# Attention and feed-forward in one kernel: copies of the weights issued earlier, sums of weights stored in fewer transfers, and a planned order made anew

## The chip, the core and the metric

The kernel runs on one core of a Trainium2 chip. The metric is device time in microseconds (us). The kernel before takes 865.53 us, the median of three runs (864.79 to 868.05).

## What is computed

Eight batches of attention with linear cost (softmax of q over its features, softmax of k over the sequence), eight heads of 64 features, 576 tokens. Its result is the input x (4608 x 512) of a feed-forward part with squared relu.

```python
q_s = exp(q - max(q, axis=-1));  q_s = q_s / sum(q_s, axis=-1)
k_s = exp(k - max(k, axis=2));   k_s = k_s / sum(k_s, axis=2)
kv = einsum('bhsd,bhse->bhde', k_s, v)
x = einsum('bhsd,bhde->bhse', q_s, kv)      # heads side by side: 4608 x 512
g = maximum(x @ w_in, 0) ** 2               # w_in 512 x 2048
out = g @ w_out                             # w_out 2048 x 512
```

## The kernel before, in words

**Exactness.** Each fp32 factor is split into a high and a low part (fp32r), and a product is three matmuls: high by high, low by high, high by low.

**Tiles and blocks.** The tokens make nine blocks of 512: 512 of the 576 of each batch, and a ninth of the 64 left over from each. Attention goes by pairs of heads, four to a block: `2.3` is pair 3 of block 2. Blocks 0 to 2 are multiplied plainly: step n (16 to a block, one for each chunk of 128 columns of w_in) has four pieces `h` of three matmuls each, then relu, square and split of the result (`relu`, `rm`, `ghi`, `glo`), and four pieces `o` that add to the output. Blocks 3 to 8 are taken two at a time in three wide passes `s0`, `s1`, `s2`, with seven products for each pair of chunks in place of eight (`A11`, `S4`, `S2`, `A12`, `S3`, `S1`, `A22`); the products need sums and differences of the weights and of the inputs. For a wide pass the weights don't fit beside the rest: each tile of 512 KB is read again from DRAM (`s0.R.5`, function `refill`, line 981).

**Where those copies come from.** The weights are first read in ORDER's steps. Later `own` (the unit `WA` of a pair of chunks, line 1028) stores three quarters of two w_in tiles, three transfers of 256 KB; `save` (units `W12`, `W34`, line 1020) stores the high and low parts of the sums, which DVE, POOL and ACT make before (units `a1` to `l34` of `w0` to `w7`); `keep_out` (`keep.n`, line 969) stores a w_out tile, 512 KB, 13 of them; `bring_back` (line 972) fetches four of them ahead of the first wide pass.

**One pair of heads**, units in turn: `Lk`, `Lq`, `Lv` load k, q and v; `km`, `k1`, `k2`, `ke`, `kx` and `qm`, `qd`, `qx`, `qs`, `qy` are the two softmaxes on DVE, POOL and ACT; `tb` turns q's tile on DVE, `Bw` writes it to DRAM (bounce) and `B` reads it back as qT, four DMAs into one tile; `kv` is the product of k and v; `kr` (with rs and kf), `kh` and `kl` scale and split it (kvs, ACT high, DVE low); `qh` and `ql` split qT (qs, ACT and POOL); `P0` to `P3` multiply the two, and `c`, `d`, `xh`, `xl`, `XL`, `XR` take the result as x.

**Inputs of a wide pass.** `x0.LB22` and its kin (line 1056) load half a block of x from DRAM; `x0.T10` to `x0.T41` are differences on DVE, `x0.hT2..` casts on ACT, `x0.lT2..` low parts on DVE. T1, T2, T3 use B22 or what was made of it; the product S2 uses T2.

**What sets the order.** Every engine works strictly in the order in which its instructions are written (class `InOrder`, line 284). That order is two tables of names: ORDER (from line 51) for blocks 0 and 1 and the start of 2, written by hand, and LIST (from line 91) for the rest, a planner's. All DMAs but a few are issued by SP, and an issue can't go before the ones ahead of it. `relu` and `square` (lines 876, 883) test BEGIN (line 43): from that step on the result stays in the bank and ACT squares it; before, it goes to SBUF and DVE squares it. All engine instructions have one line, that of the helper (294 before, 295 after), so the profile is read by tiles.

Of the kernel before, what the change touches and what calls it, by code (L numbers as in the profile page):

```python
# [1301 lines left out]
```

## Time and profile before

| | |
|---|---|
| median of three runs | 865.53 us (864.79 to 868.05) |
| the profiled execution | 863.45 us |
| its span on the core | 861.7 us |
| TensorE (PE) busy | 97% of the span |
| VectorE (DVE), ScalarE (ACT), GpSimd (POOL) busy | 64%, 57%, 33% |
| DMA, mean | 209 GB/s |
| TensorE's granted clock | 0.999 of full speed |

1.75 us of the profiled execution lie outside the span, and it is 2.08 us shorter than the median of the runs. In the profile's rows PE is TensorE's matmul, PEld its weight load, SPq the issue of DMAs by SP. An arrow points from input to output: `kvs<-kf` writes kvs from kf. A time in brackets is idle time before an instruction, with what ended it.

### The profile page before, as it was taken

What the parts mean: (1) busy time and instruction counts of PE and PEld (TensorE: products, weight loads), DVE (VectorE), ACT (ScalarE), POOL (GpSimd) and SP (SyncE); (2) the same over time, 40 slices, a digit from 0 to 9 for tenths busy, and PEclk for the clock granted to TensorE, in tenths of its full rate; (3) what the DMA queues carried; (4) which work ended last, traced back from release to release, by engine and by line L of the source; (5) the groups of instructions that cost most, each with busy time, mean ns of one, the idle gap of its engine ahead of it and who ended that gap; (6) DMA issues with size and microseconds to landing.
All of it is one profiled execution on the core that took longest, in us unless ns stands there. A gap on an engine that the chain in (4) does not pass through costs nothing.

```text
span 861.7 us, 13013 instructions
## 1 busy us (share of the span) xinstructions
PE 838.3 (97%) x4286; PEld 677.9 (79%) x4286; DVE 552.3 (64%) x1155; ACT 491.9 (57%) x932; POOL 288.0 (33%) x275
## 2 busy tenths in 40 slices
...
GB/s 232 294 167 310 202 75 151 273 231 277 225 231 245 271 267 289 233 301 253 252 265 263 278 173 170 236 175 168 147 242 198 102 215 147 166 162 161 175 70 49
DMA packets 136819, 179.66 MB, mean 209 GB/s; under 512 B 50864, under 2 KB 103088, under 8 KB 136752
## 3 DMA queue, kind: packets, MB, share of 16 engines
...
## 4 chain that ended last, share of the span: by engine, by line
PE 73%; DVE 10%; DMA 6%; SPq 4%; issue 3%; ACT 2%; POOL 1%; DVEq 0%; POOLq 0%; ACTq 0%
PE bank L294 73%; SPq L294 4%; DVE m L294 2%; DMA qt<-in_q_dram 1%; DMA raw_o<-in_moe_w_out_dram 1%; DMA kt<-in_k_dram 1%; DVE g_lo L294 1%; DMA xl_B<-x_raw 1%; DVE qm L294 1%; POOL qn L294 1%; DMA vt<-in_v_dram 1%; ACT bank L294 1%; DMA raw_i<-in_moe_w_in_dram 1%; DVE w L294 1%; DVE qs L294 1%
## 5 line engine op out<-in xcount | busy, mean ns | idle before, releaser
L294 PE MATMUL bank<-wp,g 128*128 128x512 f32 x648 | 160.8, 390 | 0.0
L294 PEld LDWEIGHTS bank<-wp,g 128*128 128x128 f32 x648 | 120.8, 188 | 25.3
L294 PE MATMUL bank<-x_hi,wi 128*128 128x512 f32 x384 | 131.8, 398 | 0.2 <-DVE g_lo L294 0.2
L294 PE MATMUL bank<-xh_T,wp 128*128 128x512 f32 x384 | 131.5, 392 | 0.0
L294 PE MATMUL bank<-wo,g_hi 128*128 128x512 f32 x384 | 121.0, 396 | 0.0
L294 POOL TENSOR_TENSOR qs<-qT,qs 64x640 fp32r<-64x640 f32 (+1 forms) x40 | 64.2, 1604 | 107.8 <-ACT qs L294 88.3
L294 PE MATMUL bank<-xh_B,wp 128*128 128x512 f32 x288 | 97.9, 390 | 0.0
L294 DVE TENSOR_TENSOR c<-c,bank 128x512 f32<-128x512 f32 x48 | 33.0, 687 | 95.8 <-ACT c L294 95.7
L294 PEld LDWEIGHTS bank<-x_hi,wi 128*128 128x128 f32 x384 | 72.2, 188 | 16.9 <-DVE g_lo L294 0.6
L294 ACT ACTIVATE far<-far 128x512 f32<-128x512 f32 x96 | 60.5, 631 | 42.7 <-DVE far L294 41.4
L294 PEld LDWEIGHTS bank<-xh_T,wp 128*128 128x128 f32 x384 | 72.1, 188 | 16.2 <-ACT bank L294 1.0
L294 PEld LDWEIGHTS bank<-wo,g_hi 128*128 128x128 f32 x384 | 69.8, 188 | 14.5 <-ACT g_hi L294 0.4
L294 PE MATMUL bank<-wo,g_lo 128*128 128x512 f32 x192 | 75.3, 392 | 0.0
L294 PE MATMUL bank<-x_lo,wi 128*128 128x512 f32 x192 | 75.0, 391 | 0.0
L294 PE MATMUL bank<-xl_T,wp 128*128 128x512 f32 x192 | 74.8, 390 | 0.0
L294 PE MATMUL bank<-wo_back,g 128*128 128x512 f32 x288 | 72.0, 391 | 0.0
L294 DVE TENSOR_TENSOR far<-far,bank 128x512 f32<-128x512 f32 x48 | 32.8, 684 | 50.5 <-PE bank L294 50.2
L294 DVE TENSOR_TENSOR g<-far,g 128x512 fp32r<-128x512 f32 x48 | 36.8, 806 | 43.9 <-ACT g L294 43.8
L294 PEld LDWEIGHTS bank<-xh_B,wp 128*128 128x128 f32 x288 | 54.1, 188 | 11.6
L294 PEld LDWEIGHTS bank<-wo_back,g 128*128 128x128 f32 x288 | 53.5, 188 | 11.3
L294 PE MATMUL bank<-xl_B,wp 128*128 128x512 f32 x144 | 56.2, 390 | 0.0
L294 POOL TENSOR_TENSOR qn<-qn,qs 128x640 f32<-128x640 f32 x30 | 38.2, 1274 | 52.1 <-DVE qs L294 28.9
(136 smaller groups left out, 1521.3 us busy)
## 6 DMA issues: line engine op xcount, KB each, us to landing
wp<-w_prod SPq DMA_DIRECT2D x84, 512.0 KB, 4.2
wp<-w_outs SPq DMA_DIRECT2D x54, 512.0 KB, 4.3
...
raw_i<-in_moe_w_in_dram SPq DMA_DIRECT2D x16, 512.0 KB, 6.1
raw_o<-in_moe_w_out_dram SPq DMA_DIRECT2D x16, 512.0 KB, 7.3
...
qT<-bounce SPq DMA_DIRECT2D x96, 80.0 KB, 2.9
w_outs<-wo SPq DMA_DIRECT2D x13, 512.0 KB, 3.6
```

Of the source, the lines that this page charges most:

```text
L294: ins = f(*args, **kwargs)
```

## The change

It has four parts. (1) BEGIN goes from 18 to 16, so the results of steps 16 and 17 are squared by ACT in the bank instead of by DVE in SBUF. (2) The copy of w_in gets another layout: own chunks in `w_own`, sums in `w_sums`, where high and low parts of two sums lie so that one DMA stores the high and one the low parts; a refill of a w tile then is two DMAs of 256 KB instead of one of 512 KB. (3) ORDER gets the units WA0 to WA5 and eight `ko` (keep_out) among the steps of block 1 and 2's start, and some output copies and stores (`ev`, `S`) stand earlier. (4) LIST is made anew. The units WA0 to WA7 and all 13 `keep` remain in LIST.

```diff
-BEGIN = 18
+BEGIN = 16
...
-rr13 kvn13 s2i13 rm11 lowo14 Lv21 to11 o8_2 o9_2 ghi10 ghi11 h12_0:0 h12_1 h12_2 h12_3 rc13 qmul13 s1o11 s2o11 ti14
+rr13 kvn13 s2i13 rm11 lowo14 Lv21 WA0 WA1 to11 o8_2 o9_2 ghi10 ghi11 h12_0:0 h12_1 h12_2 h12_3 rc13 qmul13 s1o11
...
-h15_2 h15_3 Lv22 ghi13 relu14 to14 s1o14 s2o14 to15 glo13 o13_3 o13_1 o13_2 hio14 loo14 o13_0 s1o15 s2o15 hio15 rm14
-ghi14 glo14 h16_0:1 relu15 rm15 ghi15 glo15 Bw20 Lk23 o14_3 qsub21 at13:3 loo15 o15_3 xhi13 xlo13 o14_0 o15_0 B20
-rs20 h16_1 rr20 qexp21 qn21 ev0 Bw21 h16_2 o14_1 o15_1 ev1 qh20 ql20 kf20 h16_3 relu16 rm16 B21 ev3 o14_2 o15_2 ev2
-ghi16 S2 glo16 Lq23 kh20 kl20 S0 S3 h17_0:3 h17_1 h17_2 h17_3 S1 relu17 rm17 ghi17 glo17
+h15_0:3 h15_1 h15_2 h15_3 Lv22 WA2 WA3 ko0 ko1 ko2 ghi13 relu14 to14 s1o14 s2o14 to15 glo13 o13_3 o13_1 o13_2 hio14
+loo14 o13_0 s1o15 s2o15 hio15 rm14 ghi14 glo14 h16_0:1 relu15 rm15 ghi15 glo15 Bw20 Lk23 WA4 ko3 ko4 ko6 ko7 o14_3
+qsub21 at13:3 loo15 o15_3 xhi13 xlo13 o14_0 o15_0 B20 rs20 h16_1 rr20 qexp21 ev3 S3 qn21 ev0 S0 WA5 ko8 Bw21 h16_2
+o14_1 o15_1 ev1 qh20 ql20 kf20 h16_3 relu16 rm16 ghi16 S1 B21 glo16 o14_2 o15_2 ev2 S2 kh20 kl20 Lq23 h17_0:3 h17_1
+h17_2 h17_3
...
 LIST = """
-P0/2.0 qm/2.2 w0.a2 w0.WA h18_0 c0/2.0 h18_1 d0/2.0 qd/2.2 km/2.2 P1/2.0 h18_2 c1/2.0 h18_3 d1/2.0 w0.s1 Lq/3.0
+w0.a2 w0.s1 qm/2.2 P0/2.0 h18_0 relu17 km/2.2 qd/2.2 h18_1 rm17 h18_2 ghi17 c0/2.0 h18_3 glo17 qx/2.2 o.16.0 d0/2.0
...
-    w_prod = dram.tile([len(used) // 2, P, 2, 2, 2 * P], F32, name="w_prod")
+    w_own = dram.tile([NPR, P, 3, 2, 2 * P], F32, name="w_own")
+    w_sums = dram.tile([NPR, 2, P, 2, 2, 2 * P], F32, name="w_sums")
...
         if kind == "w":
-            e.sp.dma_start(t.bitcast(F32), w_prod[i])
-            for k in range(2):
-                held[s, used[2 * i + k]] = t[:, k]
+            for k, (j, name) in enumerate(used[2 * i : 2 * i + 2]):
+                held[s, (j, name)] = t[:, k]
+                if name[0] == "A":
+                    src = w_own[j, :, ("A11", "A12", "A22").index(name)]
+                else:
+                    n, m = divmod(int(name[1]) - 1, 2)
+                    src = w_sums[j, n, :, :, m]
+                e.sp.dma_start(t[:, k].bitcast(F32), src)
...
         def save(n, src):
-            for i in range(2):
-                pair, place = divmod(w_at[j, f"S{2 * n + i + 1}"], 2)
-                e.sp.dma_start(w_prod[pair, :, place, 0], m[n][:, i].bitcast(F32))
-                e.sp.dma_start(w_prod[pair, :, place, 1], m[src][:, i])
+            e.sp.dma_start(w_sums[j, n, :, 0], m[n].bitcast(F32))
+            e.sp.dma_start(w_sums[j, n, :, 1], m[src])
...
+    parts = {f"w{j}": sum_units(j) for j in range(NPR)}
+    for j in range(NPR):
+        units[f"WA{j}"] = parts[f"w{j}"]["WA"]
+    for fc in range(NFC):
+        units[f"ko{fc}"] = lambda fc=fc: keep_out(fc)
     for token in ORDER:
```

How the change moves instructions, at three places. The rows are an engine's instructions in their order, each with its line, output, inputs and shape; "x4" is four alike in a row.

*SP at the end of ORDER*, from the v loads of block 2's third pair to the second fetch of qT. Before:

```order
L294 DMA vt_80<-in_v_dram 64x4x64
L294 DMA bounce<-tb 128x640
L294 DMA kt_79<-in_k_dram 64x2x320
L294 DMA kt_79<-in_k_dram 64x2x256
L294 DMA qT<-bounce 32x4x160 x4
L294 DMA bounce<-tb 128x640
L294 DMA qT<-bounce 32x4x160 x4
L294 DMA out_dram<-o 64x512 x2
```

In the changed kernel (the rows up to the stores after the first fetch):

```order
L295 DMA w_outs<-wo_713 128x1024
L295 DMA bounce<-tb 128x640
L295 DMA kt_79<-in_k_dram 64x2x320
L295 DMA kt_79<-in_k_dram 64x2x256
L295 DMA w_own<-wi_994 128x2x256 x2
L295 DMA w_own<-wi_1063 128x2x256
L295 DMA w_outs<-wo_798 128x1024
L295 DMA w_outs<-wo_878 128x1024
L295 DMA w_outs<-wo_1023 128x1024
L295 DMA w_outs<-wo_1094 128x1024
L295 DMA qT<-bounce 32x4x160 x4
L295 DMA out_dram<-o 64x512 x4
```

Ahead of the rows shown of the changed kernel, behind the v loads, stand six more stores of w_own and two of w_outs (WA2, WA3, ko0, ko1). So sixteen stores of weights now stand between the v loads and the first fetch of qT.

*SP at the start of LIST*, from the first q loads on. Before:

```order
L294 DMA w_prod<-wi_385 128x2x256 x2
L294 DMA w_prod<-wi_405 128x2x256
L294 DMA qt_82<-in_q_dram 64x2x320
L294 DMA qt_82<-in_q_dram 64x2x256
L294 DMA x_left<-xf 128x2x32
L294 DMA w_prod<-wi_494 128x2x256 x2
L294 DMA w_prod<-wi_507 128x2x256
L294 DMA w_prod<-wi_993 128x2x256 x2
L294 DMA w_prod<-wi_1062 128x2x256
L294 DMA bounce<-tb 128x640
L294 DMA vt_81<-in_v_dram 64x5x64
L294 DMA vt_81<-in_v_dram 64x4x64
```

In the changed kernel:

```order
L295 DMA w_outs<-wo_1266 128x1024
L295 DMA w_outs<-wo_1375 128x1024
L295 DMA w_outs<-wo_656 128x1024
L295 DMA w_outs<-wo_1479 128x1024
L295 DMA w_outs<-wo_596 128x1024
L295 DMA bounce<-tb 128x640
L295 DMA w_outs<-wo_1509 128x1024
L295 DMA w_outs<-wo_1576 128x1024
L295 DMA qt_83<-in_q_dram 64x2x320
L295 DMA qt_83<-in_q_dram 64x2x256
L295 DMA w_outs<-wo_713 128x1024
L295 DMA w_outs<-wo_798 128x1024
```

In place of weight copies spread between the loads, the w_outs stores of all 13 keeps (nine are among these rows) stand close together; the first w_own store of LIST comes behind the next fetch of qT.

*DVE ahead of the first wide pass*: the differences T, their low parts xl_T and what stands between them. Names end in the number of a buffer. Before, the last of them:

```order
L294 TENSOR_TENSOR xl_B_3034<-xl_B_3034,xh_B_3157 128x512
L294 TENSOR_TENSOR T_3853<-xl_B_3697,xl_T_3447 128x512
L294 TENSOR_TENSOR xl_T_3794<-T_3831,xh_T_3734 128x512
L294 TENSOR_TENSOR g_lo<-bank_92,g_hi 128x512
L294 TENSOR_TENSOR T_3881<-xl_B_3697,T_3831 128x512
L294 TENSOR_TENSOR T_3886<-xl_B_3202,T_3881 128x512
L294 TENSOR_TENSOR xl_T_3447<-T_3853,xh_T_3758 128x512
L294 TENSOR_SCALAR rs<-bank_89 128x1
L294 RECIPROCAL rs<-rs 128x1
L294 TENSOR_SCALAR kf<-bank_89,rs 128x64
L294 TENSOR_TENSOR xl_T_3837<-T_3881,xh_T_3766 128x512
```

In the changed kernel, the twelve from the first one that uses B22 (T_3875) to the low part of T2's second half:

```order
L295 TENSOR_TENSOR T_3875<-xl_B_3805,xl_T_3709 128x512
L295 TENSOR_TENSOR T_3881<-xl_B_3805,T_3836 128x512
L295 TENSOR_TENSOR T_3893<-xl_B_3265,T_3881 128x512
L295 TENSOR_TENSOR xl_T_3709<-T_3875,xh_T_3883 128x512
L295 TENSOR_TENSOR xl_T_3905<-T_3881,xh_T_3891 128x512
L295 TENSOR_TENSOR T_3911<-xl_T_3709,xl_B_2863 128x512
L295 TENSOR_TENSOR xl_B_2863<-xl_B_2863,xh_B_3546 128x512
L295 TENSOR_TENSOR T_3926<-xl_B_3805,xl_T_3709 128x512
L295 TENSOR_TENSOR xl_T_3855<-T_3911,xh_T_3850 128x512
L295 TENSOR_TENSOR g_lo<-bank_92,g_hi 128x512
L295 TENSOR_TENSOR T_3952<-xl_B_3805,T_3911 128x512
L295 TENSOR_TENSOR xl_T_3905<-T_3952,xh_T_3891 128x512
```

Before, work of a pair of heads (rs, kf) and of steps stands between them, and the first use of B22 lies 26 rows ahead of the last one shown; now they follow one another, with one g_lo among them.

## Rows read from the trace of the kernel before

**Rows 1.** The page, part 1: busy time, share of the span, instructions.

```profile
PE 838.3 (97%) x4286; PEld 677.9 (79%) x4286; DVE 552.3 (64%) x1155; ACT 491.9 (57%) x932; POOL 288.0 (33%) x275
```

**Rows 2.** Windows: length, busy us (instructions) by engine; clock, DMA share, GB/s.

```profile
120.00:140.00 20.00, 18.60 (x78) 14.03 (x76) 17.48 (x26) 8.91 (x17) 7.47 (x5) 1.00 0.24 71
...
215.00:335.00 120.00, 111.10 (x604) 88.56 (x603) 93.48 (x223) 68.91 (x142) 70.36 (x71) 1.00 0.85 255
...
500.00:520.00 20.00, 17.72 (x93) 13.88 (x93) 18.34 (x31) 6.82 (x15) 9.16 (x7) 1.00 0.53 145
```

**Rows 3.** Chain of waits, 215 to 335 us, shares by line.

```profile
by line: SPq L294 25.5%; issue 11.2%; PE bank L294 9.1%; DMA kt<-in_k_dram 6.5%; DVE m L294 5.3%; DMA xl_B<-x_raw 4.8%; DMA vt<-in_v_dram 4.1%; DMA w_prod<-s 3.5%; DVE g_lo L294 3.2%; POOL s L294 2.5%; POOL qn L294 2.1%; DMA out_dram<-o 2.0
```

**Rows 4.** Timeline of SP, 240 to 272 us: start, length, what, how many.

```profile
244.54 2.56 SPq L294 DMA_DIRECT2D vt<-in_v_dram  x4
...
260.51 0.48 SPq L294 DMA_DIRECT2D w_prod<-s  x1
261.04 0.46 SPq L294 DMA_DIRECT2D w_prod<-w_sum  x1
```

**Rows 5.** Timeline, 227 to 301 us, DVE and PE; in brackets idle time before, releaser.

```profile
228.15 1.33 DVE L294 TENSOR_REDUCE m<-kt 128x128 f32<-128x640 f32 x1 [3.65 <-DMA kt<-in_k_dram]
...
235.53 0.42 PE L294 MATMUL bank<-qs,kvs 128*128 128x320 f32 x1 [1.53 <-DVE kvs L294]
...
262.55 0.85 PE L294 MATMUL bank<-qs,kvs 128*128 128x320 f32 x3 [0.85 <-ACT kvs L294]
...
269.74 1.32 DVE L294 TENSOR_REDUCE m<-kt 128x128 f32<-128x640 f32 x1 [3.63 <-DMA kt<-in_k_dram]
...
270.29 0.80 PE L294 MATMUL bank<-vt,kt 128*64 128x65 f32 x20 [2.39 <-ACT kt L294]
...
297.50 1.26 DVE L294 TENSOR_REDUCE m<-kt 128x128 f32<-128x640 f32 x1 [3.01 <-DMA kt<-in_k_dram]
...
299.94 0.93 PE L294 MATMUL bank<-qs,kvs 128*128 128x320 f32 x3 [1.73 <-ACT kvs L294]
```

**Rows 6.** DMA issues: count, KB each, median us from issue to landing.

```profile
wp<-w_prod SPq DMA_DIRECT2D x84, 512.0 KB, 4.2
...
qT<-bounce SPq DMA_DIRECT2D x96, 80.0 KB, 2.9
...
xl_B<-x_raw SPq DMA_DIRECT2D x8, 512.0 KB, 5.8
```

**Rows 7.** Windows: one store of a w_out tile alone.

```profile
166.50:168.00 1.50, 1.50 (x9) 0.97 (x7) 0.96 (x2) 1.45 (x3) 1.15 (x3) 1.00 1.00 378
```

**Rows 8.** Timeline, 127 to 142 us, around the LIST's start.

```profile
129.11 1.75 SPq L294 DMA_DIRECT2D qT<-bounce  x4
...
132.01 1.48 ACT L294 CAST qs<-qT 64x640 fp32r<-64x640 f32 x2
...
132.87 3.67 POOL L294 TENSOR_TENSOR qs<-qT,qs 64x640 fp32r<-64x640 f32 x2 [6.17 <-ACT qs L294]
...
136.04 0.39 PE L294 MATMUL bank<-x_lo,wi 128*128 128x512 f32 x1
...
138.08 0.39 PE L294 MATMUL bank<-x_lo,wi 128*128 128x512 f32 x1
...
140.50 0.39 PE L294 MATMUL bank<-qs,kvs 128*128 128x320 f32 x1 [1.80 <-ACT kvs L294]
```

**Rows 9.** Timeline of PE, 513 to 520 us.

```profile
515.64 0.38 PE L294 MATMUL bank<-qs,kvs 128*128 128x320 f32 x1 [1.73 <-DVE kvs L294]
...
518.66 0.38 PE L294 MATMUL bank<-qs,kvs 128*128 128x320 f32 x1 [0.55 <-DVE xf L294]
```

**Rows 10.** Groups by line and form: count, busy us, mean ns, idle before.

```profile
L294 ACT ACTIVATE bank<-bank 128x512 f32<-128x512 f32 x60 | 34.9, 582 | 17.0 <-PE bank L294 15.9
...
L294 DVE TENSOR_TENSOR T<-xl_B,T 128x512 f32<-128x512 f32 x12 | 8.2, 686 | 0.1
...
L294 DVE TENSOR_TENSOR r<-r 128x512 f32<-128x512 f32 x2 | 2.5, 1232 | 0.4 <-ACT r L294 0.4
```

More of the change, by code (lines that the diff above doesn't have):

```diff
@@ new lines @@
+x0.lT10 h47_0 ghi46 ke/5.1 h47_1 glo46 s0.R.3 h47_2 x0.hB220 x0.T30 XL/4.2 h47_3 x0.T20 x0.hT30 o.45.0 s0.R.4
+x0.hT20 x0.T40 o.45.1 x0.lT30 x0.hT40 o.45.2 relu47 x0.lT20 o.45.3 rm47 x0.T11 o.46.0 s0.R.5 ghi47 x0.lB111 o.46.1
+x0.hT11 x0.T31 o.46.2 o.46.3 x0.lT11 x0.hT31 s0.0.A11 x0.hB221 x0.pT40 glo47 back.0 o.47.0 x0.T21 x0.pB210 x0.hT21
+s0.0.c1 back.1 ev.2.0.a x0.lT21 st.2.0 x0.T41 s0.0.S2 kx/5.1 x0.lT31 x0.hT41 km/5.2 x0.pB211 s0.R.7 s0.0.u2 x0.pT41
+k1/5.2 s0.0.A12 B/5.0 k2/5.2 x0.pB220 o.47.1 s0.0.r11 s0.0.S3 x0.pB221 s0.0.m11 back.2 ev.2.1.d s0.0.S1 s0.R.8
@@ new lines @@
+qx/5.2 Lv/5.3 kp/5.1 kr/5.1 qs/5.2 kh/5.1 s0.o.1.2 s0.o.1.3 s0.1.a22 qy/5.2 s0.1.A22 s0.1.rf1 s0.R.13 kl/5.1
+s0.1.qf1 Lk/5.3 tb/5.2 s0.o.2.0 s0.1.r21 s0.o.2.1 qd/5.3 s0.1.m21 Bw/5.2 s0.o.2.2 qm/6.0 s0.1.h1 s0.o.2.3 Lq/6.1
+qx/5.3 s0.1.l1 s0.2.A11 qs/5.3 s0.R.15 s0.1.S4 s0.2.c1 s0.R.14 qy/5.3 km/5.3 s0.o.3.0 s0.1.a12 s0.2.S2 k1/5.3
+s0.1.rf0 B/5.1 s0.2.A12 s0.2.u2 k2/5.3 s0.1.qf0 s0.o.3.1 s0.2.r11 s0.R.16 s0.2.S3 s0.2.m11 s0.2.h0 s0.2.S1 s0.R.17
+s0.2.u3 s0.2.l0 qh0/5.1 ke/5.3 s0.o.3.2 s0.2.a22 ql0/5.1 kx/5.3 s0.o.3.3 back.3 tb/5.3 qh1/5.1 s0.2.A22 qm/6.1
@@ new lines @@
+s0.4.hf1 s0.o.22.2 s0.4.lf1 x1.LB22 s0.o.22.3 k2/7.0 qd/7.1 s0.o.23.0 s0.o.23.1 qx/7.1 Lq/7.3 x1.T10 s0.o.23.2
+x1.lB110 x1.hT10 s0.o.23.3 x1.lT10 s1.R.0 s0.o.24.0 s0.5.hf0 s0.o.24.1 s0.5.lf0 s0.5.hf1 s0.o.24.2 x1.hB220 s0.5.lf1
+s0.o.24.3 x1.hB221 x1.LB21 x1.T30 s0.o.25.0 x1.T20 x1.hT30 s0.o.25.1 x1.lT30 x1.hT20 s0.o.25.2 s1.R.1 x1.lT20
+s0.o.25.3 x1.pB220 s0.o.26.0 s0.6.hf0 s0.o.26.1 s0.6.hf1 s1.R.2 s0.6.lf0 s0.o.26.2 x1.hB210 s0.6.lf1 s0.o.26.3
+x1.hB211 x1.T40 s0.o.27.0 s1.R.3 x1.T11 x1.hT40 s0.o.27.1 x1.lB111 x1.hT11 s0.o.27.2 x1.T31 s0.o.27.3 B/7.0 x1.lT11
@@ new lines @@
+s0.o.28.0 s0.7.hf0 s0.o.28.1 s0.7.lf0 s0.7.hf1 s0.o.28.2 x1.hT31 s1.R.4 s0.7.lf1 s0.o.28.3 x1.lT31 s0.o.29.0 k1/7.1
+x1.pT40 s0.o.29.1 qh0/7.0 s0.o.29.2 qh1/7.0 x1.T21 s0.o.29.3 x1.T41 x1.hT21 s0.o.30.0 s1.R.5 x1.lT21 x1.hT41
+s0.o.30.1 qs/7.1 x1.pB210 s0.o.30.2 s0.o.30.3 ke/7.0 s1.0.A11 x1.pB211 k2/7.1 kx/7.0 s0.o.31.0 s1.0.c1 x1.pT41
+kv/7.0 qm/7.3 ev.4.0.a s1.0.S2 Lv/7.2 ke/7.1 kp/7.0 s1.0.A12 kr/7.0 x1.pB221 s1.0.u2 kx/7.1 s0.o.31.1 ql0/7.0 s1.R.7
+s1.0.r11 s1.0.S3 s1.0.m11 Lk/7.2 ev.4.1.d ql1/7.0 s1.0.h0 s1.0.S1 s1.0.u3 st.4.0 kh/7.0 s1.0.l0 s0.o.31.2 st.4.1
@@ L963, in attention_ffn_kernel @@
             tiles_of.append((kind, n))
-    w_prod = dram.tile([len(used) // 2, P, 2, 2, 2 * P], F32, name="w_prod")
+    w_own = dram.tile([NPR, P, 3, 2, 2 * P], F32, name="w_own")
+    w_sums = dram.tile([NPR, 2, P, 2, 2, 2 * P], F32, name="w_sums")
     w_outs = dram.tile([NFC, P, 2, NT], F32, name="w_outs")
-    w_at = {u: i for i, u in enumerate(used)}
     held, wo_at, back = {}, {}, {}
@@ L1020, in save @@
         def save(n, src):
-            for i in range(2):
-                pair, place = divmod(w_at[j, f"S{2 * n + i + 1}"], 2)
-                e.sp.dma_start(w_prod[pair, :, place, 0], m[n][:, i].bitcast(F32))
-                e.sp.dma_start(w_prod[pair, :, place, 1], m[src][:, i])
+            e.sp.dma_start(w_sums[j, n, :, 0], m[n].bitcast(F32))
+            e.sp.dma_start(w_sums[j, n, :, 1], m[src])
         def own():
             one, two = wi[2 * j], wi[2 * j + 1]
-            for name, t in (("A11", one[:, :, : 2 * P]), ("A12", one[:, :, 2 * P :]), ("A22", two[:, :, 2 * P :])):
-                pair, place = divmod(w_at[j, name], 2)
-                e.sp.dma_start(w_prod[pair, :, place], t.bitcast(F32))
+            for i, t in enumerate((one[:, :, : 2 * P], one[:, :, 2 * P :], two[:, :, 2 * P :])):
+                e.sp.dma_start(w_own[j, :, i], t.bitcast(F32))
         return dict(
@@ L1228, in attention_ffn_kernel @@
                 pairs[b, pr] = attention(b, pr, True)[1]
-    parts = {}
     def run(token):
@@ L1236, in run @@
         elif kind[0] == "w":
-            j = int(kind[1:])
-            if kind not in parts:
-                parts[kind] = sum_units(j)
             parts[kind][args[0]]()
```

350 lines of the change are left out of this document (165 added, 185 removed).

## The prediction

> **What bounds the kernel now.** I read the page first: TensorE is busy 97% of the span [rows 1], so an edit that leaves its 4286 matmuls alone, as this one does, can win back only its idle time. The windows by stage say where that is: 8.9 us between 215 and 335 us (120.00 less 111.10), 2.3 us between 500 and 520, and a single 1.8 us at 140.50, where the planned stretch (the LIST) begins [rows 2, 8]. Most of the rest is in the first 22 us, and at the end after the last matmul, where nothing here reaches. So some 13 us are open to this change.
>
> What makes TensorE wait between 215 and 335? The chain of waits of that stretch has the issue of DMAs by SP in first place, 25.5%, and the loads kt, vt and xl_B behind it [rows 3]. SP's timeline shows one issue right after another: four pieces of vt take 2.56 us, each small store of a sum of weights 0.46 to 0.48 [rows 4]. Then the engines: DVE waits 3.65, 3.63 and 3.01 us for a kt load; DVE works in order, so behind that reduce sit the small products that scale kf and kvs, and TensorE's waits of 1.53, 2.39 and 1.73 us follow [rows 5]. With the 0.85 us at 262.55 the four longest waits make 6.50 of the 8.9 us. The reader should see a late load, not a slow engine.
>
> **The change part by part.**
>
> *Fewer issues by SP.* Each of 16 pairs of sums is stored in two transfers instead of four: 32 issues fewer, at 0.46 us [rows 4] 14.7 us of SP, nearly all between the LIST's start and 335 us. Times in the LIST are sums of TensorE's own work up to there, 0.68 us for a piece of three matmuls (138.08 less 136.04 is three pieces [rows 8]). Between 75 and 190 us of it eight keeps of w_out and three bring-backs go, eleven units of 512 KB, and three weight copies, 4.5 units, come: 3.4 MB less of the 30.6 MB that 255 GB/s makes of 120 us [rows 2].
>
> *The LIST made anew.* It places q, k and v loads and qT fetches by other times. I take away the four longest waits of the stretch, 6.5 us, and leave the small ones (2.4 us), since kl still stands within a piece of the P0 that needs it. Bounds: 0, if they only move, and 8.9.
>
> *At 515 us*, TensorE waits 1.73 us for kvs and 0.55 for xf [rows 9]; DVE is busy 18.34 of 20 us there [rows 2], with x1's chain ahead of kl/7.0. The new LIST has no kl in that chain. I let the long wait shrink to the short one: −1.2 (bounds −2.3 and 0).
>
> *Copies in ORDER.* Between block 2's second set of v loads and the qT fetch that was issued at 129.11 [rows 8] stand nine transfers of 256 KB and seven of 512 KB: 11.5 units of 512 KB. A window in which only such a store moved shows 378 GB/s [rows 7], thus 1.39 us a unit, 16.0 us in all; the copies WA0 and WA1 before, and WA5 and ko8 behind, add less. DMA is idle enough (share 0.24 from 120 to 140 us [rows 2]), but its own work and these together run some 4 us past 129. So qT lands near 136 instead of 132.0. Its casts began at 132.01, POOL's subtracts ended at 136.54 (132.87 and 3.67); both go on by 4 us, to 140.5, and P0 had to wait for kvs until 140.50 anyway [rows 8]. I count 0. From below: ev3 and S3 now stand ahead of the fetch, DVE loses a square r<-r just before kvs, so the 1.80 us may vanish. From above: at the stretch's 255/0.85 = 300 GB/s [rows 2] a unit takes 1.75 us, 20 us in all, and P0 is 3 us late.
>
> *BEGIN from 18 to 16.* Steps 16 and 17: two DVE squares of 1.23 us out, two ACT passes of 0.58 in [rows 10]. ACT is busy 8.91 of the 20 us before 140 [rows 2], which hides them: 0; were ACT full, 1.2 us more. DVE, at 17.48 of 20, is the one relieved.
>
> *The keeps all at once.* The copies are still in the LIST: SP's order has all 13 keeps there, though eight of them were issued in ORDER, and all eight weight copies, of which six were. So 8.9 MB more are written than before. The 13 keeps now stand within LIST times 6.8 to 19.8 us, among two q loads, one v load, three bounces and one fetch. That is 13 × 1.39 = 18.1 us of transfers and 1.8 MB of loads, 3.56 units, 5.0 us: 23.1 us, against 17.5 us until the fetch B/2.2 is due (24.3). The backlog of 5.6 us, the fetch's own landing of 2.9 [rows 6] and one cast and one subtract, 0.74 and 1.84 us [rows 8], give 35.4 us; P0/2.2 stands at 34.3. I take +1. At 1.75 us a unit it is 29.0 us, a backlog of 11.5, and P0/2.2 is 7.0 us late. With the spare DMA time all used it is 0. I take the value by the 378 GB/s row, since it shows just such a store alone.
>
> *The differences of inputs for the first wide pass.* LB22 is issued at LIST time 179.4 (before 162.1), and the product S2 that needs lT21 stands at 193.6 (194.3 before). In 14.2 us fit the load, 5.8 us [rows 6], and twelve DVE instructions of some 0.70 [rows 10], 8.4 us, and a cast of 0.62 on ACT: 14.8. DVE carries work on kt besides. I take +1.5; bounds 0, since median landings of 5.8 come from a busier queue, and 3, one late load.
>
> *Refills of w tiles in two transfers:* 84 more issues by SP of about 0.45 us, mostly after 335 us, where SP has room; refills stand 9.5 us or more ahead of their first product, and land in 4.2 [rows 6]. 0; if SP were full there, one refill late by 1 to 2 us.
>
> Sum on the profiled execution: 863.45 − 6.5 − 1.2 + 1 + 1.5 = 858.25. The runs' median lies 2.08 above that execution, so **860.3 us**.
>
> A rule that speaks against the largest term: the chain gives SP's issues 25.5% [rows 3]. The Trainium skill (DMA: Bandwidth & Descriptors, Issuing engines are not separate DMA queues) says that all issuing engines share the 16 DMA engines, and that the issue time saved "is usually small relative to the DMA itself". By that rule the first two parts give nothing (second rival); the trace speaks against it so far, with issues of 0.46 us each back to back [rows 4].
>
> **Rivals.**
>
> 1. *The doubled stores jam the queue (slower).* Mechanism: 13 keeps in a row in front of the fetch for P0/2.2, and 16 us of copies in front of the one for P0/2.0. It decides when a 512 KB store needs more than about 1.6 us beside the loads. For it: 300 GB/s was the rate over the busy stretch; against: 378 GB/s in the window of a store alone. At 1.75: +7 and +3 in place of +1, the late chain +3: 863.45 − 6.5 − 1.2 + 10 + 3 = 868.75, with 2.08 **870.8**.
>
> 2. *SP isn't the limit; waits only move (no change).* The LIST was made by other costs than those of the chip, and a new order finds new late loads: the fetches B now stand 4 to 7 us ahead of their cast, before 6 to 12. For it: each long wait was one load, and DMA was at 0.85. Then −6.5 becomes 0: 864.75, with 2.08 **866.8**.
>
> 3. *Everything goes.* 8.9, 2.3 and 1.8 us are all won, with nothing late in their place: 863.45 − 13.0 = 850.5, with 2.08 **852.5**. Against it: the small waits in the stretch belong to the order kl, P0, which stays.
>
> 4. *The change doesn't do what it says.* By SP's order this is partly so: the copies are issued early and again. It costs nothing of its own beyond the first rival.
>
> **How the numbers follow.** What can be told from no change is about 0.5%, 4.3 us: under 861.2 is faster, above 869.9 slower. Forecast 0.48: with the spread of its terms (about ±4) 0.29 of it under 861.2, 0.18 within, 0.01 above. Rival 1 0.20, of which 0.16 above 869.9; rival 2 0.19 (0.02, 0.15, 0.02); rival 3 0.13, all faster. Together 0.44, 0.37, 0.19. The range from 852 to 871 leaves out half of rival 3 and the tail of rival 1. Where the forecast alone holds, it would be 856 to 865.
>
> **What would show it.** Right: TensorE's idle time between 215 and 335 us falls from 8.9 to about 2.4 us, SP's issues come off the first place of that chain, and DVE's 3 us idle on kt are gone. At 140.5 us still a wait under 2 us; near 175 us one of about 1 us on a cast or subtract of qs; near 335 us one of 1 to 2 us before the first wide products. Rival 1 shows as waits of 3 us and more at 140 and 175 us, behind qT<-bounce. Rival 2 shows as 6 us or more of waits in the same stretch on kvs or kt, with SP less busy. Wrong altogether: a stage that runs longer without a wait, or waits after 520 us, where there are none now.

## The result, and the profile after

The changed kernel takes 856.13 us (median of four runs, 855.1 to 857.68); the kernel before took 865.16 beside it. The ratio is 0.9895, 95% interval 0.9862 to 0.9929: faster, by 9 us. The forecast was 860.3 us in a range of 852 to 871, faster with a chance of 0.44. The direction and the range held, but the sum came out by errors in both directions. The experiments show that the change is made of two parts, worth 9 and 11 us alone and 16 together, and a third that gives 7 of them back.

First the waits of TensorE over the whole span, after (what it waited for; us in total, times, longest). The 1.4, 1.3 and 0.2 us for DVE qs, x_hi and qn lie in the first 22 us, as before.

```profile
PE bank L295 <- DVE kvs L295: 3.8, 1, 3.8
PE bank L295 <- POOL kt L295: 1.5, 1, 1.5
PE bank L295 <- ACT kvs L295: 1.4, 1, 1.4
PE bank L295 <- DVE qs L295: 1.4, 1, 1.4
PE bank L295 <- POOL x_hi L295: 1.3, 1, 1.3
PE bank L295 <- ACT bank L295: 1.1, 1, 1.1
PE bank L295 <- DVE xr L295: 1.1, 1, 1.1
PE bank L295 <- POOL qn L295: 0.2, 1, 0.2
```

The windows of the changed kernel that answer to [rows 2], with 140 to 215 us besides:

```profile
120.00:140.00 20.00, 18.59 (x78) 14.01 (x76) 15.13 (x27) 9.65 (x18) 6.11 (x5) 1.00 0.98 339
140.00:215.00 75.00, 69.62 (x367) 56.02 (x368) 58.40 (x136) 46.49 (x97) 43.13 (x46) 0.98 0.85 276
215.00:335.00 120.00, 120.00 (x671) 98.09 (x670) 93.50 (x225) 69.91 (x144) 66.05 (x69) 1.00 0.81 242
...
500.00:520.00 20.00, 20.00 (x105) 16.35 (x104) 16.73 (x36) 11.35 (x19) 10.26 (x8) 1.00 0.39 115
```

Between 215 and 335 us TensorE is now busy 120.00 of 120.00 us, and 20.00 of 20.00 from 500 to 520: the 8.9 and 2.3 us of before are gone entirely. But from 140 to 215 us it is idle 5.4 us. The chain of waits of the stretch from 215 to 335 us, the answer to [rows 3], shows the same:

```profile
by line: PE bank L295 87.9%; DMA xl_B<-x_raw 4.9%; DVE T L295 3.6%; DVE xl_B L295 1.4%; DVE xl_T L295 1.0%; SPq L295 0.7%; issue 0.6%; DVE g_lo L295 0.1%; DVEq L295 0.0%
```

SP's issues, 25.5% of that chain before, are 0.7%; TensorE's own matmuls are 87.9%. DVE's waits for kt there are 1.4 us in all, before 12.7. The new waits stand elsewhere. The timeline of the changed kernel, 140 to 422 us, the rows of SP, ACT and TensorE that matter:

```profile
140.09 0.38 PE L295 MATMUL bank<-qs,kvs 128*128 128x320 f32 x1 [1.40 <-ACT kvs L295]
...
150.57 4.41 SPq L295 DMA_DIRECT2D w_outs<-wo  x5
...
155.08 1.16 SPq L295 DMA_DIRECT2D bounce<-tb  x1
...
160.41 0.39 PE L295 MATMUL bank<-qs,kvs 128*128 128x320 f32 x1 [1.47 <-POOL kt L295]
...
168.14 2.20 SPq L295 DMA_DIRECT2D w_outs<-wo  x2
...
173.27 1.84 SPq L295 DMA_DIRECT2D qT<-bounce  x4
...
176.36 0.72 ACT L295 CAST qs<-qT 64x640 fp32r<-64x640 f32 x1 [5.33 <-DMA qT<-bounce]
...
179.78 0.38 PE L295 MATMUL bank<-qs,kvs 128*128 128x320 f32 x1 [3.82 <-DVE kvs L295]
...
338.18 0.50 PE L295 MATMUL bank<-xh_T,wp 128*128 128x512 f32 x1 [1.13 <-ACT bank L295]
...
421.55 0.39 PE L295 MATMUL bank<-qs,kvs 128*128 128x256 f32 x1 [1.09 <-DVE xr L295]
```

Read it from the SP rows: the first five keeps are issued from 150.57 on, the bounce of pair 2.2 at 155.08, and only behind the other eight keeps (shown: two of them, at 168.14), a q load, a v load, the next bounce and two stores of x_left the fetch qT<-bounce, at 173.27. ACT's cast has been idle 5.33 us for it, and P0/2.2 starts at 179.78 after a wait of 3.82. P0/2.1 waited 1.47 us at 160.41. The waits at 338 (first wide products) and 421 us are 1.13 and 1.09 us.

One wait costs more than its length. Windows of TensorE's granted clock (the figure behind its busy time) around the one of 3.82 us:

```profile
170.00:175.00 5.00, 5.00 (x24) 1.00 0.89 305
...
180.00:182.00 2.00, 2.00 (x6) 0.51 0.70 201
182.00:184.00 2.00, 2.00 (x7) 0.63 0.72 201
184.00:186.00 2.00, 2.00 (x12) 1.00 1.02 311
```

TensorE ran at full clock before, was idle, and then was granted 0.51 and 0.63 in two stretches of 2 us: by these two means, some 3.5 us at 1.2 GHz instead of 2.4. That lost 2 × 0.49 + 2 × 0.37 = 1.7 us.

**Where the 7.4 us between the two spans (861.7 and 854.3) are.** For 140 to 215 us, the kernel before has these waits of TensorE:

```profile
PE bank L294 <- ACT kvs L294: 1.8, 1, 1.8
PE bank L294 <- DVE kvs L294: 1.6, 2, 0.9
```

By estimate a listed wait is short by some 0.16 us, for a matmul is shown 0.39 long while they follow each other by 0.68/3 = 0.23 [rows 8]. With that: 215 to 335 us, −8.9 − 1.6 (ten waits) = −10.5; 500 to 520, −2.3 − 0.3 = −2.6; 140 to 180, three waits of 6.7 us for three of 3.4 before, +3.3; the clock, +1.7; the two waits at 338 and 421, +2.5. Sum −5.6; where the remaining 1.8 us are is not shown. The medians lie 9.0 us apart and not 7.4, since the profiled execution of the kernel before (863.45) is 1.7 us shorter than the median beside it (865.16), while that of the changed kernel (856.13) is its median.

### The profile page after: what moved, and what is told of

Read it like the earlier page. It is cut to its first block, busy times and chain, and to the rows that moved or that the text cites. A ratio compares the mean times of both kernels' runs of the same rounds, so it can differ in the third digit from the quotient of the medians.

```text
span 854.3 us, 13089 instructions
## 1 busy us (share of the span) xinstructions
PE 837.1 (98%) x4286; PEld 679.1 (79%) x4286; DVE 548.8 (64%) x1153; ACT 494.0 (58%) x934; POOL 287.0 (34%) x275
## 4 chain that ended last, share of the span: by engine, by line
PE 84%; DVE 5%; DMA 4%; ACT 2%; issue 2%; SPq 2%; POOL 1%; DVEq 0%; ACTq 0%; POOLq 0%
PE bank L295 84%; DMA qt<-in_q_dram 2%; SPq L295 2%; DMA kt<-in_k_dram 1%; DVE m L295 1%; DMA xl_B<-x_raw 1%; DMA qT<-bounce 1%; DVE T L295 1%; DVE w L295 1%; DVE bank L295 1%; ACT bank L295 1%; DVE g_lo L295 0%; POOL qn L295 0%; ACT g_hi L295 0%; ACT qs L295 0%
## 5 line engine op out<-in xcount | busy, mean ns | idle before, releaser
L295 PEld LDWEIGHTS bank<-x_hi,wi 128*128 128x128 f32 x384 | 72.3, 188 | 16.4 <-DVE x_lo L295 0.4
L295 DVE TENSOR_TENSOR g<-far,g 128x512 fp32r<-128x512 f32 x48 | 34.0, 747 | 38.7 <-ACT g L295 38.5
L295 ACT CAST g<-far 128x512 fp32r<-128x512 f32 x48 | 27.7, 620 | 51.5 <-PE bank L295 51.2
```

What stands on the lines that cost most here:

```text
L295: ins = f(*args, **kwargs)
```

## The experiments

Each experiment was timed in five rounds beside runs of the kernel before; ratios are to it. Kernels that did not share those runs are compared by their ratios.

| kernel | median, us | ratio | 95% interval |
|---|---|---|---|
| the change | 856.13 | 0.9895 | 0.9862 to 0.9929 |
| change, no doubles in LIST | 849.75 | 0.9804 | 0.9779 to 0.9829 |
| change, only doubled keeps out of LIST | 850.39 | 0.9822 | 0.9793 to 0.9850 |
| change, no copies in ORDER | 849.05 | 0.9812 | 0.9786 to 0.9837 |
| the same, BEGIN 18 | 848.48 | 0.9806 | 0.9779 to 0.9833 |
| the same as the third, old layout | 855.71 | 0.9876 | 0.9848 to 0.9904 |
| change, old layout | 859.33 | 0.9925 | 0.9902 to 0.9949 |
| change, LIST of before | 859.51 | 0.9918 | 0.9895 to 0.9942 |
| before, new layout alone | 856.46 | 0.9897 | 0.9871 to 0.9923 |
| before, two stores, short rows | 857.21 | 0.9900 | 0.9885 to 0.9916 |
| before, four stores, short rows, split refills | 866.18 | 1.0001 | 0.9989 to 1.0014 |
| before, four stores of half the partitions | 877.18 | 1.0133 | 1.0118 to 1.0149 |
| change, four keeps early, no doubles, ACT's order | 846.44 | 0.9782 | 0.9755 to 0.9808 |

### The doubled stores

**No doubles in LIST.** The six weight copies and eight keeps that ORDER issues are struck from LIST.

```diff
 LIST = """
...
-h19_1 glo18 xh0/2.0 keep.11 h19_2 xl0/2.0 d2/2.0 keep.0 tb/2.2 h19_3 keep.12 P3/2.0 keep.1 o.17.0 qm/2.3 relu19
+h19_1 glo18 xh0/2.0 keep.11 h19_2 xl0/2.0 d2/2.0 tb/2.2 h19_3 keep.12 P3/2.0 o.17.0 qm/2.3 relu19
...
-glo21 h22_1 d3/2.1 h22_2 w0.WA ke/2.3 xh1/2.1 kv/2.2 xl1/2.1 kx/2.3 h22_3 kr/2.2 Lq/3.2 kp/2.2 o.20.0 w0.a1 relu22
+glo21 h22_1 d3/2.1 h22_2 ke/2.3 xh1/2.1 kv/2.2 xl1/2.1 kx/2.3 h22_3 kr/2.2 Lq/3.2 kp/2.2 o.20.0 w0.a1 relu22
...
```

> The changed kernel without the doubles in LIST: w0 to w5's WA and the eight keeps that ORDER already issues are taken out of LIST. Theory (the doubled stores hold up SP and the queue ahead of the qT fetches): the waits of 1.5 us at 160 and 3.8 us at 180 us go or shrink under 0.5 each, the time falls by 4 to 5.5 us, to 851 to 852. Rival (the new order itself puts that fetch too late, the stores only stand beside it): both waits stay within 1 us of their size, time within 1.5 us of 856.1.

849.75 us: 6.4 less than the change (7.9 by the ratios), more than the 4 to 5.5 that I had given it. The wait of 3.82 us is gone, but the one at 160 us is still 1.0 and not under 0.5. So the doubled stores made the long wait, as the theory has it, and only a part of the short one.

**No copies in ORDER.** The other way round.

```diff
-h15_0:3 h15_1 h15_2 h15_3 Lv22 WA2 WA3 ko0 ko1 ko2 ghi13 relu14 to14 s1o14 s2o14 to15 glo13 o13_3 o13_1 o13_2 hio14
-loo14 o13_0 s1o15 s2o15 hio15 rm14 ghi14 glo14 h16_0:1 relu15 rm15 ghi15 glo15 Bw20 Lk23 WA4 ko3 ko4 ko6 ko7 o14_3
+h15_0:3 h15_1 h15_2 h15_3 Lv22 ghi13 relu14 to14 s1o14 s2o14 to15 glo13 o13_3 o13_1 o13_2 hio14
+loo14 o13_0 s1o15 s2o15 hio15 rm14 ghi14 glo14 h16_0:1 relu15 rm15 ghi15 glo15 Bw20 Lk23 o14_3
...
```

> The changed kernel without the copies in ORDER (WA0 to WA5 and eight ko taken out there; LIST keeps all of its own). Theory (what is issued early costs nothing and, since LIST issues all of it again, brings nothing): time within 1 us of 856.1, the wait at 140 us between 1.0 and 1.8 us. Rival 1 (the early copies delay the fetch for P0/2.0 and all behind it): 1.5 to 3 us faster. Rival 2 (they take work off LIST's start): slower by 1.5 us or more.

849.05 us, 7 less. Rival 1 was right, and stronger than it was stated: the early copies, doubled in LIST, cost all that this kernel gave back. Without them, the timeline from 143 to 174 us:

```profile
143.95 5.06 SPq L295 DMA_DIRECT2D w_outs<-wo  x5
...
149.12 1.13 SPq L295 DMA_DIRECT2D bounce<-tb  x1
...
162.21 2.18 SPq L295 DMA_DIRECT2D w_outs<-wo  x2
...
167.00 2.59 SPq L295 DMA_DIRECT2D qT<-bounce  x4
...
170.45 0.73 ACT L295 CAST qs<-qT 64x640 fp32r<-64x640 f32 x1 [2.91 <-DMA qT<-bounce]
...
173.90 0.39 PE L295 MATMUL bank<-qs,kvs 128*128 128x320 f32 x1 [1.43 <-DVE kvs L295]
```

The same 13 keeps stand in the same place. But SP comes to the first of them at 143.95 instead of 150.57, 6.6 us earlier, and to the fetch at 167.00 instead of 173.27; ACT waits 2.91 us for it instead of 5.33, and P0/2.2 1.43 us instead of 3.82. No wait is left at 140 or 160 us. So the row of keeps alone costs 1.4 us; behind early copies, which bring SP to it late, it costs more. Summed up, the change has waits of 1.40, 1.47 and 3.82 us and 1.7 us of clock there, 8.4 in all, this kernel 1.43. The difference, 7.0, is what the runs measured, 7.1. Taking either set away takes away nearly all.

**Only the doubled keeps out.**

```diff
 LIST = """
...
-kx/2.2 glo19 keep.2 h20_1 keep.3 xh1/2.0 qs/2.3 qh0/2.1 xl1/2.0 Lv/2.3 h20_2 qh1/2.1 h20_3 kr/2.1 qy/2.3 o.18.0
+kx/2.2 glo19 h20_1 xh1/2.0 qs/2.3 qh0/2.1 xl1/2.0 Lv/2.3 h20_2 qh1/2.1 h20_3 kr/2.1 qy/2.3 o.18.0
...
```

> The changed kernel with only the eight doubled keeps taken out of LIST; the six doubled weight copies stay there. Theory (the row of 13 keeps ahead of the fetch for P0/2.2 is what costs, since SP enters LIST late): the waits of 1.5 us at 160 and 3.8 us at 180 us fall to 1 us or less each, and the time comes to 849 to 851.5, as without any doubles (849.75). Rival (the doubled weight copies behind that fetch cost as much): 853 to 856.5.

850.39 us, within 0.7 of the kernel without any doubles. The wait at 180 us is gone and the one at 160 us is 0.8: what the doubles cost comes from the keeps, not from the weight copies.

### Layout and order

**The layout alone** on the kernel before (the diff's w_own, w_sums, save and refill; nothing else).

```diff
-            for i in range(2):
-                pair, place = divmod(w_at[j, f"S{2 * n + i + 1}"], 2)
-                e.sp.dma_start(w_prod[pair, :, place, 0], m[n][:, i].bitcast(F32))
-                e.sp.dma_start(w_prod[pair, :, place, 1], m[src][:, i])
+            e.sp.dma_start(w_sums[j, n, :, 0], m[n].bitcast(F32))
+            e.sp.dma_start(w_sums[j, n, :, 1], m[src])
```

> The kernel before with the new layout of the copy alone (sums stored in two transfers, refills of w tiles in two). Theory (issues of SP delay the loads of the stretch 215 to 335 us): idle time of TensorE there falls from 8.9 us to 5 to 7, the time by 2 to 3.5 us. Rival (the old order puts loads where they are late anyway): idle time stays within 1 us of 8.9, time within 1.5 us of the kernel before.

856.46 us: as fast as the whole change. I had given it 2 to 3.5 us, and it is worth 9. Its chain and its window, 215 to 335 us:

```profile
by line: PE bank L294 82.6%; DMA qT<-bounce 3.0%; SPq L294 3.0%; DMA kt<-in_k_dram 2.3%; DVE m L294 2.0%; issue 1.4%; DVE a L294 1.1%; ACT bank L294 1.0%; DVE sums L294 0.6%; ACT kt L294 0.6%; DVE g_lo L294 0.5%; DVE mt L294 0.5%; DVE qs L2
```

```profile
215.00:335.00 120.00, 118.21 (x638) 96.15 (x637) 103.44 (x234) 71.90 (x147) 75.08 (x74) 0.99 0.88 269
```

SP falls to 3.0% of the chain with the old order unchanged, and idle time from 8.9 to 1.8 us. The kt loads come sooner, though not all in time: DVE waits for them 8.1 us there in place of 12.7, and behind the longest such wait stands the one wait that TensorE has left, with a lower granted clock behind it:

```profile
265.11 1.31 DVE L294 TENSOR_REDUCE m<-kt 128x128 f32<-128x640 f32 x1 [2.87 <-DMA kt<-in_k_dram]
265.62 0.80 PE L294 MATMUL bank<-vt,kt 128*64 128x65 f32 x20 [1.72 <-ACT kt L294]
```

```profile
266.00:268.00 2.00, 2.00 (x20) 0.63 0.82 250
268.00:270.00 2.00, 2.00 (x6) 0.52 0.82 124
```

**Is it the number of issues, or the rows?** One store of the new layout has rows of 2 KB where the old had 1 KB, so two mechanisms change at once. Three kernels separate them. Two stores of 256 KB that write rows of 1 KB:

```diff
-            e.sp.dma_start(w_sums[j, n, :, 0], m[n].bitcast(F32))
-            e.sp.dma_start(w_sums[j, n, :, 1], m[src])
+            e.sp.dma_start(w_sums[j, n, :, :, 0].rearrange("i p f -> p i f"), m[n].bitcast(F32))
+            e.sp.dma_start(w_sums[j, n, :, :, 1].rearrange("i p f -> p i f"), m[src])
```

> The kernel before with the new layout, but the two stores of a pair of sums write rows of 1 KB as before: two issues of 256 KB. Theory (number of issues): near the layout alone, 855 to 858. Rival (length of rows): near the kernel before, 862 to 866. Between the two if both count.

857.21 us: the whole gain, with short rows. Four stores with short rows, but refills in two:

```diff
+            for i in range(2):
+                e.sp.dma_start(w_sums[j, n, i, :, 0], m[n][:, i].bitcast(F32))
+                e.sp.dma_start(w_sums[j, n, i, :, 1], m[src][:, i])
```

> The kernel before with stores of sums in four issues of 128 KB in rows of 1 KB, as before, and only the refills of w tiles in two DMAs of 256 KB. Theory (refills in two cost nothing, the gain is the stores'): within 2 us of the kernel before, 863.5 to 867.5. Rival (the halved refills are part of the gain): 2 us or more faster.

866.18 us, no change (0.9989 to 1.0014): the split refills cost and bring nothing, and all of the layout's gain is in joining the stores. That makes 32 issues fewer, but each store also twice as large, and these two kernels can't tell the one from the other. Four stores with rows of 2 KB, each for half of the partitions:

```diff
+            for i in range(2):
+                e.sp.dma_start(w_sums[j, n, half[i], 0], m[n][half[i]].bitcast(F32))
+                e.sp.dma_start(w_sums[j, n, half[i], 1], m[src][half[i]])
```

> The kernel before with the new layout, but each store of sums cut in two by partitions: four issues of 128 KB for a pair as before, in rows of 2 KB. Theory (the number of issues by SP is what the layout saves): near the kernel before, 862 to 866, idle time between 215 and 335 us 5 us or more. Rival (rows of 2 KB in place of 1 KB make the stores shorter): near the layout alone, 855 to 858.

877.18 us, slower than before by 11 us, which neither side expected; TensorE's idle time between 215 and 335 us is 15.7 us (8.9 before). The timeline of SP in it:

```profile
241.40 0.55 SPq L294 DMA_DIRECT2D w_sums<-w_sum  x1
242.05 0.54 SPq L294 DMA_DIRECT2D w_sums<-a  x1
242.64 0.59 SPq L294 DMA_DIRECT2D w_sums<-w_sum  x1
243.28 0.63 SPq L294 DMA_DIRECT2D w_sums<-a  x1
```

and in the kernel with four stores of 128 partitions:

```profile
239.31 0.46 SPq L294 DMA_DIRECT2D w_sums<-w_sum  x1
239.86 0.40 SPq L294 DMA_DIRECT2D w_sums<-a  x1
240.36 0.41 SPq L294 DMA_DIRECT2D w_sums<-w_sum  x1
...
241.44 0.43 SPq L294 DMA_DIRECT2D w_sums<-w_sum  x1
```

The same bytes in as many stores, but an issue takes 0.54 to 0.63 us instead of 0.40 to 0.46; over all 64 the medians are 0.59 and 0.44 us. By these rows 64 issues are longer by some 0.15 us each, 9.8 us of SP, and the kernel is longer by 11.0. The joined stores took 9 us off the kernel; added up over the traces, the stores of sums take SP 28.2 us before and 16.4 with the layout alone, 11.8 fewer (an issue of the larger store is somewhat longer, so it is not the 14.7 of the prediction). So a microsecond of SP between 140 and 335 us goes with 0.8 (saved) to 1.1 us (added) of the kernel's, as long as SP is what the chain runs through.

The Trainium skill (DMA: Bandwidth & Descriptors, Rules for kernel authors) advises against splitting a transfer in partition halves, since both halves use the same 16 engines. The run agrees with the advice. The stores themselves land in the same 2.4 to 2.6 us as before, which speaks for the issue as what costs. It isn't shown to be all of it: in the chain of waits from 215 to 335 us SP has 18.1%, no more than with four stores of 128 partitions (19.5%), while the stores that read s have 9.8% instead of 3.5%.

**The order without the layout**: no early copies, old layout, so in effect the new LIST.

```diff
-    w_own = dram.tile([NPR, P, 3, 2, 2 * P], F32, name="w_own")
-    w_sums = dram.tile([NPR, 2, P, 2, 2, 2 * P], F32, name="w_sums")
+    w_prod = dram.tile([len(used) // 2, P, 2, 2, 2 * P], F32, name="w_prod")
```

> The changed kernel without early copies and with the old layout: in effect the new LIST (with BEGIN 16 and the moved output copies) alone, no store made twice. Theory (layout and order each give a part): 1.5 to 3.5 us slower than the same kernel with the new layout (849.05), so 850.5 to 852.5, the difference in the stretch 140 to 340 us. Rival 1 (the order is all): within 1 us of 849.05. Rival 2 (the order works only with SP relieved): 4 us or more slower.

855.71 us, ratio 0.9876, 6.7 us slower: rival 2's number. The new order clears most of the stretch by itself, but SP comes late with LB22: it issues that load at 320.29 us, with the new layout at 314.40, and DVE is idle 3.76 us before the first difference that uses it (the profile names a kt load, issued just behind LB22, as what ended that). Waits of TensorE in it from 215 to 345 us, and its clock behind the longest:

```profile
PE bank L295 <- DVE xl_B L295: 2.6, 1, 2.6
PE bank L295 <- DVE kvs L295: 0.9, 1, 0.9
PE bank L295 <- ACT bank L295: 0.9, 1, 0.9
```

```profile
334.00:336.00 2.00, 1.83 (x5) 0.50 1.00 399
336.00:340.00 4.00, 3.23 (x8) 0.50 0.34 87
340.00:345.00 5.00, 5.00 (x18) 0.71 0.83 204
```

The wait for xl_B, 2.6 us, stands in the chain of differences before the first wide pass; the changed kernel and the one with the new layout have none for it, only the 1.1 us for ACT. And behind it TensorE is granted half its clock for 6 us and 0.71 over the next 5. By the rows that loses 1.83 × 0.5 + 3.23 × 0.5 + 5.00 × 0.29 = 4.0 us, more than the wait itself, and over half of the 7.6 us between the two profiled spans (854.4 and 846.8). Another execution of the same kernel, at a mean granted clock of 0.999 (the profiled one has 0.992 and 856.24 us), took 852.16 us, within the theory's range: what the layout is worth in the new order depends in part on whether the clock falls. The layout takes the wait away, and the two gains together are 16 us (849.05, ratio 0.9812), not the 20 of their sum.

**The change with the old layout.**

```diff
-            e.sp.dma_start(w_sums[j, n, :, 0], m[n].bitcast(F32))
-            e.sp.dma_start(w_sums[j, n, :, 1], m[src])
+            for i in range(2):
+                pair, place = divmod(w_at[j, f"S{2 * n + i + 1}"], 2)
+                e.sp.dma_start(w_prod[pair, :, place, 0], m[n][:, i].bitcast(F32))
+                e.sp.dma_start(w_prod[pair, :, place, 1], m[src][:, i])
```

> The changed kernel with the old layout of the copy: four stores for a pair of sums, own chunks stored as before, refills of one DMA of 512 KB. Theory (SP's issues are the limit between 140 and 335 us): SP has 32 issues more, 14 us, and waits of TensorE return there, 2 to 5 us in all: 858 to 861. Rival (SP has room in the new order, its issues are small beside the transfers): within 1 us of 856.1.

859.33 us, 3.2 more, as expected, though the intervals of the two ratios overlap. The place was not the one I had named: from 215 to 335 us TensorE waits 0.4 us, but behind 335 us 2.8 us for xl_B. In the two profiled executions (861.48 and 856.13 us) the waits differ by only 1.5 us in all; the rest is mostly granted clock, 0.50 to 0.70 in the windows from 340 to 348 us. So this run doesn't show that the 32 issues cost 3.2 us by themselves.

```profile
PE bank L295 <- DVE xl_B L295: 2.8, 1, 2.8
```

**The change with the old LIST** (no doubles).

```diff
 LIST = """
-w0.a2 w0.s1 qm/2.2 P0/2.0 h18_0 relu17 km/2.2 qd/2.2 h18_1 rm17 h18_2 ghi17 c0/2.0 h18_3 glo17 qx/2.2 o.16.0 d0/2.0
+P0/2.0 qm/2.2 w0.a2 h18_0 c0/2.0 h18_1 d0/2.0 qd/2.2 km/2.2 P1/2.0 h18_2 c1/2.0 h18_3 d1/2.0 w0.s1 Lq/3.0
...
```

> The layout, BEGIN and ORDER of the change with the LIST of the kernel before, without the doubled copies in it. Theory (fewer SP issues and fewer stores clear most of the waits between 215 and 335 us, whatever the order): idle time there falls from 8.9 us to 4 or less, time 858 to 861. Rival (the planner's new order is what clears them): idle time there 6 us or more, time 862 to 866.

859.51 us: the theory's number. Idle time from 215 to 335 us is 2.3 us, with the old order. Against the layout alone (856.46) it has only the early copies, BEGIN and the moved output copies more, and it isn't faster: a new wait of 2.50 us on ACT stands at 158 us. Which of these edits brings that wait isn't separated. That the whole set of early copies doesn't pay even where nothing is doubled, the new order shows too: 849.75 us with it (no doubles in LIST), 849.05 without.

### BEGIN, and a faster version

**BEGIN 18**, without early copies.

```diff
-BEGIN = 16
+BEGIN = 18
```

> The changed kernel without early copies and with BEGIN at 18: steps 16 and 17 squared by DVE as before. Theory (this part costs and brings nothing): within 1 us of 849.05, no wait of over 0.5 us at 140 us. Rival (the DVE square ahead of kvs made the wait of 1.8 us before): a wait of 1 to 2 us at 140 us and 1 to 2 us slower.

848.48 us: no difference, as the theory said. But the rival's wait is there: 1.7 us for kvs at 140 us. In its place the wait of 1.4 us at 174 us is gone: SP issues the fetch for P0/2.2 no later (166.35 us, with BEGIN 16 167.00), while TensorE, held up at 140 us, comes to it later.

**Four keeps early, none doubled, and ACT's copy ahead of a cast.**

```diff
-loo14 o13_0 s1o15 s2o15 hio15 rm14 ghi14 glo14 h16_0:1 relu15 rm15 ghi15 glo15 Bw20 Lk23 WA4 ko3 ko4 ko6 ko7 o14_3
+loo14 o13_0 s1o15 s2o15 hio15 rm14 ghi14 glo14 h16_0:1 relu15 rm15 ghi15 glo15 Bw20 Lk23 ko4 ko6 ko7 ko8 o14_3
...
-km/2.3 relu20 o.18.1 ql0/2.1 rm20 tb/2.3 o.18.2 keep.4 kh/2.1 keep.6 o.18.3 kp/2.1 Bw/2.3 kl/2.1 h21_0 ghi20 ql1/2.1
-keep.7 P0/2.1 glo20 h21_1 keep.8 c0/2.1 h21_2 XL/2.0 d0/2.1 k1/2.3 P1/2.1 h21_3 c1/2.1 o.19.0 d1/2.1 relu21 o.19.1
+km/2.3 relu20 o.18.1 ql0/2.1 rm20 tb/2.3 o.18.2 kh/2.1 o.18.3 kp/2.1 Bw/2.3 kl/2.1 h21_0 ghi20 ql1/2.1
+P0/2.1 glo20 h21_1 c0/2.1 h21_2 XL/2.0 d0/2.1 k1/2.3 P1/2.1 h21_3 c1/2.1 o.19.0 d1/2.1 relu21 o.19.1
...
-x0.hT11 x0.T31 o.46.2 o.46.3 x0.lT11 x0.hT31 s0.0.A11 x0.hB221 x0.pT40 glo47 back.0 o.47.0 x0.T21 x0.pB210 x0.hT21
-s0.0.c1 back.1 ev.2.0.a x0.lT21 st.2.0 x0.T41 s0.0.S2 kx/5.1 x0.lT31 x0.hT41 km/5.2 x0.pB211 s0.R.7 s0.0.u2 x0.pT41
+x0.hT11 x0.T31 o.46.2 o.46.3 x0.lT11 x0.hT31 s0.0.A11 x0.hB221 x0.pT40 glo47 back.0 o.47.0 x0.T21 x0.pB210 s0.0.c1 x0.hT21 back.1 ev.2.0.a x0.lT21 st.2.0 x0.T41 s0.0.S2 kx/5.1 x0.lT31 x0.hT41 km/5.2 x0.pB211 s0.R.7 s0.0.u2 x0.pT41
```

> The changed kernel without the early copies, but with four keeps (4, 6, 7, 8) moved from LIST into ORDER, behind the k load of block 2's last pair, where DMA is idle; and ACT's copy of the first wide bank put ahead of the cast it waits behind. Nothing is stored twice. Theory (13 keeps in a row before the fetch for P0/2.2 cost 1.4 us, nine cost nothing; ACT's order costs about 0.8 us before the first wide products): the wait near 174 us goes, the one near 331 us falls from 1.1 to 0.6 or less, 846.5 to 848. Rival (four keeps behind the k load delay the fetch of qT as the whole early set did): a wait of 1 us or more at 140 us, 849 or more.

846.44 us, the fastest of all: 846.24 to 846.86 in four executions, against 848.14 to 849.31 for the kernel with BEGIN 18 that was timed beside it. Its waits of TensorE from 215 to 345 us are the only ones it has behind the first 22 us (its helper is line 294, for its LIST is one line shorter):

```profile
PE bank L294 <- POOL xl_B L294: 0.7, 1, 0.7
PE bank L294 <- ACT bank L294: 0.4, 1, 0.4
```

The waits at 140, 160 and 174 us are gone; the one on ACT's copy fell to 0.4, and 0.7 us on xl_B appeared beside it. The two edits weren't timed apart.

## Why the prediction was right, and where not

**The bound was read rightly.** The late loads behind SP's issues in [rows 3 to 5] were what held TensorE: stores joined into 32 issues fewer nearly cleared the stretch in the old order, and longer issues went with more idle time there. The Trainium skill (DMA: Bandwidth & Descriptors, Issuing engines are not separate DMA queues) says that issue time is usually small beside the transfer. For one store the rows agree, 0.46 of 2.6 us to landing; but one issue follows another, and it is their sum that held up the loads. Rival 2, which took up the same doubt, fell.

**The gain in the stretch was mis-sized.** I took 6.5 us, the four longest waits, and left 2.4 us of small ones in place because kl stands so near to its P0. All 8.9 went (rival 3's figure, and its forecast of the stretch was the right one). The small waits went with the layout alone as well, so they too hung on SP; what it leaves is 1.72 us of a long one. I also gave layout and order one gain between them. Alone they are worth 9 and 11 us (0.9897, 0.9876), together 16 (0.9812).

**At 515 us** all 2.3 us went, where I had 1.2: with no kl in that chain, the wait for xf behind it went too. It is the order that does it: with the layout alone both waits are still there (1.74 and 0.59 us).

**The copies in ORDER at 0 and the keeps at +1, added as if each stood alone: that is the step that failed.** Alone each was about right. The copies in ORDER with no doubles behind them cost nothing that can be told (849.75 against 849.05 us), and the keeps without the copies 1.4 us. I asked only whether qT for P0/2.0 would be late, and it was not (a wait of 1.40 us at 140.09, before 1.80). But SP came out of ORDER with a backlog, and I costed the keeps from LIST's own times, as if SP entered LIST on time. It reached them 6.6 us later than it does without the early copies. Both had to be added in one queue: together they make 3.3 us more waits than before and 1.7 us of clock, which I had not thought of, 5.0 us in place of +1.

**Rival 1** had that mechanism, for 175 us: 3.82 us there. At 140 us, where it named 3 us and more too, the wait was 1.40. Its price was 10 us, twice what came, and its condition, stores at 300 GB/s, didn't hold: from 150 to 156 and 156 to 162 us, with stores beside loads, DMA moves 350 and 388 GB/s. The row of 378 GB/s that I held against it [rows 7] was itself not a store alone, as I had read it: SP issues three stores of w_prod from 166.06 us on, in the same window.

**Chain before the first wide products:** +1.5 forecast, 1.13 measured. **BEGIN** and **split refills:** 0 forecast, no difference measured in either. **Not forecast:** 1.09 us at 421 us, where DVE is idle 2.71 us for a kt load just ahead; without the copies in ORDER the same LIST has no wait there.

**Luck in the sum.** The profiled execution was forecast at 858.25 us and took 856.13. The stretch and 515 us gave 3.5 us more than I had by the listed waits, the copies and keeps took 4.0 more, 1.1 at 421 us stood in no term, and some 3.4 us of the gain lie in no listed wait. To this I had added 2.08 us, because the kernel before was that much slower in the median than in its profiled execution; the changed kernel was not, and this makes half of the 4.2 us by which 860.3 is off.

**Rival 4** was certain from the order of instructions, and I gave it no price of its own. The stores made twice cost 6 to 8 us behind the copies in ORDER, nearly half of what the rest of the change gained.
